# Four changes to the opening of a fused attention and two-layer feed-forward kernel

## The chip, the core and the metric

The kernel runs on one core of a Trainium2 chip. Its engines are TensorE (PE in the profile; PEld is its weight load), VectorE (DVE), ScalarE (ACT), GpSimd (POOL) and SyncE (SP), which here only issues DMAs. The metric is the device time of one execution in microseconds (us). Fewer are better.

## What is computed

Four batches of eight heads of attention with a learned decay, 576 positions of 64, then two feed-forward blocks over the 2304 tokens.

```python
def attention(q, k, v, f):                       # (4, 8, 576, 64), f: (4, 8, 576)
    scores = (1 / sqrt(64)) * (q @ k.T)
    cum = cumsum(log(clip(f, 1e-4, 1)))          # running sums along the sequence
    scores = where(causal, -1e9, scores + cum[:, None] - cum[None, :])
    attn = exp(scores - max(scores))
    return (attn / (sum(attn) + 1e-9)) @ v

x = attention(q, k, v, f)                        # as 2304 tokens x 512
h = ((x @ w1) * (x @ w2)) @ w3                   # 512 -> 1024 -> 1024
x = h @ w_out                                    # 1024 -> 512
h = x @ w_in                                     # 512 -> 2048
out = (h - tanh(h)) @ w_out2                     # 2048 -> 512
```

The weights arrive as float64, so each weight unit has to be turned to float32 on the chip, and each large product is made of three matmuls on a high and a low part of both sides.

## The kernel before, in words

Every step is declared to a planner (`Plan`, `declare`) with its engine, an assumed duration, what it reads and writes and a priority `pr`; the planner runs through them once and writes out one fixed order for each engine. The priorities come from the table `C` (line 38) through `PR`: `a0` to `a3` place the 16 attention pairs, `o0`, `o1`, `w0`, `w1`, `v0`, `v1` the weight units of the first layer, `s0`, `s1` those of the second layer that are converted ahead and spilled to DRAM, `b0` the last eight. Instructions of an engine run in that order, and SP's DMAs too: a DMA that has to wait holds those behind it.

*Running sums.* Line 219 on: `f` for 32 heads is loaded on 32 partitions, clipped, passed through the logarithm and summed by a scan into the tile `PT`; line 240 writes the 32 rows to the DRAM tile `cumd`.

*Attention.* A pair is two heads of a batch (`pair`, `scores`). For each pair SP loads q and k (`qk`, line 356, two buffers), V (`VF`, line 465, two buffers) and the running sums of each head, broadcast from `cumd` to 128 partitions (`cumb`, line 358, one buffer for each head). The scores of a head are five row blocks, each up to the diagonal, in four groups of matmuls (`smm`, line 373). DVE adds the sums and takes the minimum of a row (`smin`, line 388), ACT takes the exponential (line 393), PE transposes (line 444), ACT copies the result out of PSUM (line 449), and PE multiplies by V (line 493). The causal mask is made in two ways: for pairs below `nm` = 9 by two or one more matmuls a row block and head, of the tables `eye` and `trh` (18 a pair), and from pair 9 on by GpSimd, which adds the table `tri` to the diagonal blocks of `cumb` (line 378, ten a pair).

*Weight units.* `conv` (from line 290) turns one unit, 128x512, from float64 to float32: SP loads 512 KB into a raw buffer (`w64`, line 299), ACT takes the absolute of one half (line 309), DVE makes four steps on it (lines 314 to 320), ACT rounds the high part (line 337), and the low part is a subtraction (line 340) on the engine that `lo_eng` names. The first 40 units are those of the first layer: 8 of `wo`, 16 of `w3`, 16 of `w1` and `w2`. With `lod` = 1, the first has its low part on DVE, the others on GpSimd. The raw buffers are a ring of `NW` = 2; with `xu` = 0 the four more that lie in tiles idle at first (`f`, and the second halves of `xy`) are not used. The second and third unit wait for the write of `cumd` (`h0` = 1).

*Matrix work.* `mphase` multiplies `w3` and `wo` into one matrix (192 matmuls of 512 columns), `block1` makes the first layer in six blocks of 384 tokens, between the attention of batches 1, 2 and 3, and the rest is the second layer in five blocks. In the first layer's time the attention of later pairs is woven between.

Of the kernel before, what the change touches and what calls it, by code (L numbers as in the profile page):

```python
# [37 lines left out]
C = {"nb": 4, "nm": 9, "gs": 0.4, "xs": 4, "xu": 0, "wl": 8.0, "h0": 1, "ys": 0.15, "a0": 4.51, "a1": 30.92, "a2": 85.05, "a3": 48.14, "o0": 1.62, "o1": 3.44, "w0": 22.93, "w1": 6.0, "m0": 138.47, "v0": 144.48, "v1": 5.72, "s0": 1059.48, "s1": 9.02, "lod": 1, "evd": 11, "b0": 1268.43, "k0": 1009.76}  # L38
# [32 lines left out]
class Plan:  # L71
# [8 lines left out]
    def op(self, eng, dur, fn, r=(), w=(), pr=0.0, grp=None, after=(), pn=128, use=1.0, lk=False, mode="f", lat=0.0):  # L80


        if eng == "S":
            i = self._op("S", 0.52 if pn == 128 else 0.69, fn, r, w, pr, grp, after)
            return self._op("Q", dur / 360e3 * (128 / max(pn, 64) if pn > 8 else 1), None, r, w, pr, grp, (i,))
        return self._op(eng, dur, fn, r, w, pr, grp, after, use, lk or eng == "P", mode, lat)
# [21 lines left out]
    def schedule(self):  # L108
# [19 lines left out]
        while done < n:  # L128
# [21 lines left out]
            if e == "E":  # L150
                if o["mode"] != mode:
                    t, mode = t + 0.1, o["mode"]
# [48 lines left out]
def declare(P, nc, T, a):  # L201

    op = P.op
# [42 lines left out]
    def consts(z):  # L246
        t = T["J"][:, 128 * z:128 * z + 128] if z < 2 else T["J"][:, 256:512]
        if z == 0:
            G.memset(t, 1.0)
            G.affine_select(t, t, pattern=[[1, 128]], compare_op=ALU.is_equal, fill=0.0, base=0, channel_multiplier=-1)  # L250
        elif z == 1:
            G.memset(t, 0.0)
            G.affine_select(t, t, pattern=[[-1, 128]], compare_op=ALU.is_ge, fill=-1e30, base=0, channel_multiplier=1)
        elif z == 2:
            V.tensor_copy(T["idr"], T["J"][:, 0:128])
        elif z == 3:
            V.tensor_copy(T["tri"], T["J"][:, 128:256])
        elif z == 4:
            V.tensor_copy(T["eye"][0:64, 64:128], T["J"][0:64, 0:64])
            V.tensor_copy(T["eye"][64:128, 64:128], T["J"][64:128, 64:128])  # L260
        elif z == 5:
            V.tensor_copy(T["trh"][0:64], T["J"][0:64, 128:256])
            V.tensor_copy(T["trh"][64:128, 0:64], T["J"][64:128, 192:256])
        elif z == 6:
            V.tensor_copy(T["trh"][64:128, 64:128], T["J"][64:128, 256:320])
        elif z == 7:
            G.memset(t[:, 0:64], -1e30)
            G.memset(t[:, 64:128], 0.0)
        else:
            V.tensor_copy(T["eye"][:, 0:64], T["J"][:, 320:384])  # L270
            V.tensor_copy(T["eye"][:, 128:192], T["J"][:, 320:384])

    for z in range(2):
        op("P", 0.7, lambda z=z: consts(z), w=[f"J.{z}", "J"], pr=-100, grp="att")
        op("D", 0.2, lambda z=z: consts(2 + z), r=[f"J.{z}"], w=["J", ("idr", "tri")[z]], pr=-98, grp="att")
    op("P", 0.4, lambda: consts(7), w=["J.2", "J"], pr=-100, grp="att")
    op("D", 0.3, lambda: consts(4), r=["J.0"], w=["J", "eye"], pr=-98, grp="att")
    op("D", 0.3, lambda: consts(5), r=["J.1"], w=["J", "trh"], pr=-98, grp="att")
    op("D", 0.15, lambda: consts(6), r=["J.2"], w=["J", "trh"], pr=-98, grp="att")
    op("D", 0.3, lambda: consts(8), r=["J.2"], w=["J", "eye"], pr=-98, grp="att")  # L280
# [3 lines left out]
    cnt = [0, 0]  # L284
    borrowed = []
    NW = 2

    def conv(unit, hi, lo, pr, spill=None, reload=None, lo_eng="P", grp=None):
# [63 lines left out]
    def scores(p, t0, o):  # L352
# [3 lines left out]
        o("S", 589824, lambda: Y.dma_start(T[qk], a["qk"][p]), t0 - 20, w=[qk])  # L356
        for y in range(2):
            o("S", 294912, lambda y=y: Y.dma_start(T[f"cumb{y}"], T["cumd"][h + y:h + y + 1].to_broadcast([128, S])), t0 - 8 + 2 * y, r=["cumd"], w=ck[y])
        pem = p < C["nm"]

        def smm(banks, pieces):
            for i, c0, c1, at in pieces:
                d = 128 * i - c0
                n = min(128, S - 128 * i)
                ops = [(lambda k: k[:, :, :].rearrange("p a b -> p (a b)")[:, 128 * i:128 * i + 128], lambda k: k[:, 1, c0:c1], 0, c1 - c0, qk)]
# [4 lines left out]
                for z, (l, r, f, w, src) in enumerate(ops):  # L370
                    for y in range(2):
                        sl = slice(64 * y, 64 * y + 64)
                        E.matmul(T[banks[y]][:, at + f:at + f + w], l(T[src])[sl], r(T[src])[sl], start=z == 0, stop=z == len(ops) - 1)  # L373
# [459 lines left out]
```

## Time and profile before

| | us |
|---|---|
| median of 3 runs | 966.0 (965.81 to 968.46) |
| the profiled execution | 968.27 |
| its span, first to last instruction | 966.6 |
| PE busy in it | 940.6 |
| DVE busy | 630.3 |
| ACT busy | 532.3 |
| POOL busy | 264.1 |

The profile is of one execution. Busy time counts a wait of a matmul inside the array as well, so PE's share is an upper bound of what it does. A row of the timeline gives start and duration of an instruction, or of several alike that are merged; a row of the chain gives start, duration and what was on the path that ended last. The span is 1.7 us shorter than the time of the execution that it is from.

### The profile page before, as it was taken

The numbers are of one execution on the slowest core, as the hardware profiler recorded it, in microseconds if no ns is written. First come the engines' busy times: TensorE is split into PE (matmuls) and PEld (weight loads), VectorE is DVE, ScalarE is ACT, GpSimd is POOL, SyncE is SP. The second block draws the span as 40 slices with busy tenths as digits, with TensorE's granted clock in tenths as the row PEclk, the third lists the DMA queues.
The fourth block names the chain that finished last, engine by engine and source line by source line (L and its number), as shares of the span: only waits on it lengthen the run. The fifth ranks groups of instructions, "written<-read, shape, count | busy, mean of one in ns | idle before, by whom it ended". The sixth has DMA issues, their size and how long they took to land.

```text
span 966.6 us, 14863 instructions
## 1 busy us (share of the span) xinstructions
PE 940.6 (97%) x5314; PEld 797.6 (83%) x5314; DVE 630.3 (65%) x1332; ACT 532.3 (55%) x1170; POOL 264.1 (27%) x251
## 2 busy tenths in 40 slices
PE   5799999999999999999999999999999999999998
PEld 3466777988888988899999988888888888888898
DVE  6698888886777664326422369677568666756675
ACT  4676676665564554433324465655556555655564
POOL 0322332321211111102124457242225223222221
PEclk9999999999999999999999999999999999999999
DMA  5656554546557652003113331011001000100010
GB/s 181 226 182 212 183 188 162 190 152 226 194 195 258 214 184 68 30 13 95 58 58 96 99 120 55 1 44 43 1 1 35 32 1 0 44 1 1 1 44 23
DMA packets 38666, 94.50 MB, mean 98 GB/s; under 512 B 4608, under 2 KB 8832, under 8 KB 38592
## 3 DMA queue, kind: packets, MB, share of 16 engines
q1 hardware_dynamic: 38592, 93.56, 29.0%
q8 instruction: 41, 0.67, 0.3%
q14 instruction: 33, 0.27, 0.1%
HBM read 77.67 MB, written 15.88 MB: 97 GB/s over the span
## 4 chain that ended last, share of the span: by engine, by line
PE 89%; DMA 6%; DVE 2%; ACT 1%; issue 1%; SPq 0%; ACTq 0%; DVEq 0%
PE b L207 26%; PE b L208 25%; PE b L209 25%; PE b L373 5%; PE b L444 4%; PE b L493 3%; DMA w<-in_w_dram 2%; DMA w<-in_wo_dram 1%; DMA rb<-dr 1%; DMA w<-in_win_dram 1%; DMA cumb<-cumd 1%; DMA cumd<-PT 1%; ACT w L309 0%; DVE P L388 0%; DVE w L318 0%
## 5 line engine op out<-in xcount | busy, mean ns | idle before, releaser
L683 POOL TENSOR_TENSOR s<-xy,s 128x512 fp32r<-128x512 f32 (+1 forms) x80 | 99.4, 1243 | 256.3 <-ACT s L682 242.5
L674 DVE SCALAR_TENSOR_TENSOR xy<-b,xy 128x512 f32<-128x512 f32 (+1 forms) x80 | 50.8, 635 | 114.4 <-ACT xy L673 113.2
L679 ACT ACTIVATE xy<-xy,small 128x512 f32<-128x512 f32 (+1 forms) x80 | 54.6, 682 | 79.8 <-DVE xy L678 79.6
L373 PE MATMUL b<-qk 64*128 64x512 f32 (+4 forms) x384 | 80.9, 498 | 11.4 <-DVE small L388 5.7
L449 ACT COPY PT<-b 128x512 f32<-128x512 f32 (+3 forms) x144 | 60.3, 444 | 50.0 <-PE b L444 49.6
L393 ACT ACTIVATE P<-P,small 128x512 f32<-128x512 f32 (+3 forms) x128 | 71.1, 557 | 29.2 <-DVE small L388 28.8
L378 POOL TENSOR_TENSOR cumb<-cumb,tri 128x128 f32<-128x128 f32 (+1 forms) x70 | 35.6, 513 | 162.3 <-DVE small L388 122.0
L682 ACT CAST s<-xy 128x512 fp32r<-128x512 f32 (+1 forms) x80 | 46.1, 577 | 60.3 <-DVE xy L681 60.3
L388 DVE CUSTOM_DVE_ANT_0 P<-b,cumb 128x512 f32<-128x512 f32 (+3 forms) x128 | 60.0, 483 | 24.0 <-PE b L373 22.4
L559 DVE TENSOR_TENSOR f<-b,f 128x384 f32<-128x384 f32 x48 | 26.5, 553 | 71.0 <-PE b L209 65.5
L309 ACT ACTIVATE w<-w 128x512 f32<-128x512 f32 x72 | 48.5, 673 | 36.9 <-DMA w<-in_wo_dram 16.6
L681 DVE COPY_PREDICATED xy<-xy 128x512 f32<-128x512 uint32 (+1 forms) x80 | 61.5, 769 | 9.3 <-ACT xy L679 2.4
L678 DVE SCALAR_TENSOR_TENSOR xy<-xy 128x512 f32<-128x512 f32 (+1 forms) x80 | 65.5, 818 | 0.0
L680 DVE SCALAR_TENSOR_TENSOR xy<-xy 128x512 f32<-128x512 f32 (+1 forms) x80 | 60.3, 754 | 6.8
L314 DVE TENSOR_SCALAR w<-w 128x512 f32<-128x512 f32 x72 | 33.6, 466 | 45.9 <-ACT w L309 45.3
L444 PE MATMUL b<-idr,P 128*128 128x128 f32 x320 | 53.2, 285 | 8.2 <-ACT PT L449 4.6
L373 PEld LDWEIGHTS b<-qk 64*128 64x128 f32 x384 | 35.3, 198 | 30.0 <-issue 8.9
L444 PEld LDWEIGHTS b<-idr,P 128*128 128x128 f32 x320 | 39.3, 144 | 24.6 <-ACT PT L449 11.5
L672 ACT ACTIVATE xy<-b 128x512 f32<-128x512 f32 (+1 forms) x80 | 44.5, 556 | 26.7 <-PE b L209 25.8
L318 DVE SCALAR_TENSOR_TENSOR w<-w,w 128x512 uint32<-128x512 uint32 x72 | 56.0, 779 | 1.0
L676 ACT ACTIVATE xy<-xy,small 128x512 f32<-128x512 f32 (+1 forms) x80 | 54.7, 683 | 0.0
L320 DVE SCALAR_TENSOR_TENSOR w<-w,w 128x512 uint32<-128x512 uint32 x72 | 53.5, 746 | 0.7
(630 smaller groups left out, 2839.8 us busy)
## 6 DMA issues: line engine op xcount, KB each, us to landing
w<-in_wo_dram SPq DMA_DIRECT2D x24, 512.0 KB
qk<-in_qk_dram SPq DMA_DIRECT2D x16, 576.0 KB
cumb<-cumd SPq DMA_DIRECT2D x32, 288.0 KB
w<-in_w3t_dram SPq DMA_DIRECT2D x16, 512.0 KB
w<-in_w_dram SPq DMA_DIRECT2D x16, 512.0 KB
w<-in_win_dram SPq DMA_DIRECT2D x16, 512.0 KB
VF<-in_v_dram SPq DMA_DIRECT2D x16, 320.0 KB
rb<-dr SPq DMA_DIRECT2D x32, 144.0 KB
```

The costliest lines, as they stand in the source:

```text
L207: E.matmul(o, lh, rh, start=start, stop=False)
L208: E.matmul(o, lh, rl, start=False, stop=False)
L209: E.matmul(o, ll, rh, start=False, stop=stop)
L373: E.matmul(T[banks[y]][:, at + f:at + f + w], l(T[src])[sl], r(T[src])[sl], start=z == 0, stop=z == len(ops) - 1)
L388: V.tensor_tensor_reduce(out=out, in0=T[b][0:qn, at:at + c1 - c0], in1=T[cum][0:qn, c0:c1], scale=-0.125, scalar=3e38, op0=ALU.add, op1=AL ...
L393: A.activation(t, t, AF.Exp, bias=T["MX"][:, z:z + 1], scale=-1.0, accum_out=T["SM"][:, z:z + 1])
L444: E.transpose(T[tb][0:n, 128 * z:128 * z + 128], T[src][:, c:c + n], T["idr"].bitcast(F32))
L449: (A.copy if ev == "A" else V.tensor_copy)(out(), src)
L678: op("D", d_dve(nb), lambda w=w, u=u, v=v, nb=nb: V.scalar_tensor_tensor(v(w), v(u), -P_ROOT, v(w), ALU.add, ALU.mult), r=[u], w=[w], lk=T ...
L680: op("D", d_dve(nb), lambda w=w, vv=vv, v=v, nb=nb: V.scalar_tensor_tensor(v(w), v(vv), P_D, v(w), ALU.add, ALU.mult), r=[vv], w=[w], lk=T ...
L681: op("D", d_dve(nb), lambda w=w, u=u, th=th, v=v, nb=nb: V.copy_predicated(v(w), v(u).bitcast(U32), v(th)), r=[u, th], w=[w], lk=True, **pa)
L683: op("P", d_pool(nb), lambda w=w, gh=gh, gl=gl, v=v, nb=nb: G.tensor_sub(v(gl), v(w), v(gh)), r=[w, gh], w=[gl], pr=pa["pr"], after=[*pa[" ...
```

## The change

It replaces the planner's constants and makes four changes to the program.

The two broadcasts of pair 0 read the running sums from `PT` in SBUF, one partition each, instead of from `cumd`; the loads of q and k for pair 1 and of V for pairs 0 and 1 are put behind them in SP's order (`held`). The first 20 weight units use a ring of six raw buffers (`xu` = 20, `xs` = 4), and no unit waits for the sums any more. The masks of all pairs are made by GpSimd with a select on the diagonal blocks of `cumb`; the mask matmuls, and the tables `tri`, `eye` and `trh`, are gone. The low parts of the first 40 units are all on DVE (`lod` = 40). The planner's own assumptions change too: a broadcast counts 2.7 times its bytes, the queue has 400 instead of 360 GB/s, a change of matmul type costs 0.17 instead of 0.1 us.

```diff
-C = {"nb": 4, "nm": 9, "gs": 0.4, "xs": 4, "xu": 0, "wl": 8.0, "h0": 1, "ys": 0.15, "a0": 4.51, "a1": 30.92, "a2": 85.05, "a3": 48.14, "o0": 1.62, "o1": 3.44, "w0": 22.93, "w1": 6.0, "m0": 138.47, "v0": 144.48, "v1": 5.72, "s0": 1059.48, "s1": 9.02, "lod": 1, "evd": 11, "b0": 1268.43, "k0": 1009.76}
+C = {"nb": 4, "gs": 0.928, "xs": 4, "xu": 20, "wl": 8.0, "h0": 3, "ys": 0.2, "a0": 3.061, "a1": 18.261, "a2": 74.699, "a3": 41.761, "o0": 1.714, "o1": 3.421, "w0": 22.93, "w1": 8.714, "m0": 145.732, "v0": 91.41, "v1": 4.532, "s0": 1167.053, "s1": 10.311, "lod": 40, "evd": 11, "b0": 1479.445, "k0": 1009.76}
...
-            return self._op("Q", dur / 360e3 * (128 / max(pn, 64) if pn > 8 else 1), None, r, w, pr, grp, (i,))
+            return self._op("Q", qx * dur / 400e3 * (128 / max(pn, 64) if pn > 8 else 1), None, r, w, pr, grp, (i,))
...
+    held = []
...
-            op("S", 524288, load, w=[k64], pr=pr - C["wl"], grp="w64", after=(cumw,) if C["h0"] < cnt[0] < 4 else ())
+            op("S", 524288, load, w=[k64], pr=pr - C["wl"], grp="w64", after=held if C["h0"] < cnt[0] < 4 else ())
...
-        o("S", 589824, lambda: Y.dma_start(T[qk], a["qk"][p]), t0 - 20, w=[qk])
+        o("S", 589824, lambda: Y.dma_start(T[qk], a["qk"][p]), t0 - 20, w=[qk], after=held if p == 1 else ())
         for y in range(2):
-            o("S", 294912, lambda y=y: Y.dma_start(T[f"cumb{y}"], T["cumd"][h + y:h + y + 1].to_broadcast([128, S])), t0 - 8 + 2 * y, r=["cumd"], w=ck[y])
-        pem = p < C["nm"]
+            if p:
+                o("S", 294912, lambda y=y: Y.dma_start(T[f"cumb{y}"], T["cumd"][h + y:h + y + 1].to_broadcast([128, S])), t0 - 8 + 2 * y, r=["cumd"], w=ck[y], qx=2.7)
+            else:
+                held.append(len(P.ops))
+                o("S", 294912, lambda y=y: Y.dma_start(T[f"cumb{y}"], T["PT"][y:y + 1, 0:1, 0:S].to_broadcast([1, 128, S])), -300 + y, r=ok, w=ck[y], qx=2.7)
...
-                if pem and c1 > 128 * i:
-                    ops.append((lambda k: k[:, 64:192], lambda k: T["trh"][:, 0:n], d, n, "eye"))
-                    if n > 64:
-                        ops.append((lambda k: k[:, 0:128], lambda k: T["trh"][:, 0:64], d + 64, 64, "eye"))
...
-            G.tensor_tensor(t, t, T["tri"].bitcast(F32)[0:qn, 0:qn], op=ALU.add)
+            G.affine_select(t, t, pattern=[[-1, qn]], compare_op=ALU.is_ge, fill=-1e30, base=0, channel_multiplier=1)
...
-                    if (i, c0) != (4, 0) and not pem:
-                        o("P", 0.55, lambda y=y, i=i: mask(y, i), ty, r=["tri"], w=[ck[y][i]])
+                    if (i, c0) != (4, 0):
+                        o("P", 0.32, lambda y=y, i=i: mask(y, i), ty, w=[ck[y][i]])
...
-        o("S", 327680, lambda: Y.dma_start(T[VF], a["v"][p]), -12, w=[VF])
-
         scores(p, -2.0, o)
+        o("S", 327680, lambda: Y.dma_start(T[VF], a["v"][p]), -12, w=[VF], after=held if p < 2 else ())
```

## Rows read from the trace of the kernel before

**Rows 1.** The page's part 1: busy us (share of the span) xinstructions.
```profile
PE 940.6 (97%) x5314; PEld 797.6 (83%) x5314; DVE 630.3 (65%) x1332; ACT 532.3 (55%) x1170; POOL 264.1 (27%) x251
```

**Rows 2.** Stages: stretch, its length, busy us of each engine, clock, DMA, GB/s.
```profile
core 0: us, PE busy (x) PEld busy (x) DVE busy (x) ACT busy (x) POOL busy (x), PEclk, DMA share, GB/s
0.00:75.00 75.00, 55.89 (x369) 38.42 (x370) 56.50 (x172) 48.25 (x123) 16.81 (x21) 0.98 0.58 196
75.00:200.00 125.00, 122.31 (x801) 95.86 (x801) 109.09 (x269) 86.05 (x218) 36.48 (x26) 1.00 0.55 183
200.00:450.00 250.00, 249.47 (x1610) 219.40 (x1607) 151.98 (x426) 124.24 (x326) 42.32 (x76) 1.00 0.44 148
```

**Rows 3.** PE's waits in the whole span: us in total, times, longest.
```profile
PE b L373 <- DVE small L388: 5.7, 2, 5.5
PE b L373 <- DMA qk<-in_qk_dram: 5.6, 1, 5.6
```

**Rows 4.** The timeline's first 26 us: start, duration, engine, line, operation.
```profile
1.08 0.29 POOL L250 TENSOR_SCALAR_AFFINE_SELECT J<-J 128x128 f32<-128x128 f32 x1
...
6.08 0.33 SPq L240 DMA_DIRECT2D cumd<-PT  x1
...
9.69 0.43 DVE L316 TENSOR_SCALAR w<-w 128x512 uint32<-128x512 uint32 x1
10.15 0.69 DVE L318 SCALAR_TENSOR_TENSOR w<-w,w 128x512 uint32<-128x512 uint32 x1
...
10.97 0.81 SPq L358 DMA_DIRECT2D cumb<-cumd  x2
...
12.25 0.69 DVE L340 TENSOR_TENSOR A0l<-w,A0h 128x512 fp32r<-128x512 f32 x1 [0.68 <-ACT A0h L337]
14.44 0.68 DVE L388 CUSTOM_DVE_ANT_0 J<-b,cumb 64x512 f32<-64x512 f32 x1 [1.49 <-DMA cumb<-cumd]
...
16.32 0.68 DVE L388 CUSTOM_DVE_ANT_0 J<-b,cumb 64x512 f32<-64x512 f32 x1 [0.58 <-DMA cumb<-cumd]
...
25.19 1.23 PE L373 MATMUL b<-qk 64*128 64x512 f32 x2
```

**Rows 5.** The stages' view of 5 to 10 us, columns as in rows 2.
```profile
5.00:10.00 5.00, 4.05 (x12) 1.87 (x12) 1.77 (x6) 1.01 (x3) 0.00 (x0) 1.00 0.90 326
```

**Rows 6.** The page's part 3: the DMA queue's packets, MB and share.
```profile
q1 hardware_dynamic: 38592, 93.56, 29.0%
```

**Rows 7.** Waits of DVE and of ACT from 0 to 200 us.
```profile
DVE w L314 <- ACT w L309: 13.7, 15, 3.2
...
ACT w L309 <- DMA w<-in_wo_dram: 7.8, 5, 3.2
```

**Rows 8.** The stages' view of line 340 alone: DVE busy, POOL busy.
```profile
0.00:75.00 75.00, 0.69 (x1) 15.48 (x11) 0.98 0.58 196
75.00:200.00 125.00, 0.00 (x0) 36.48 (x26) 1.00 0.55 183
```

**Rows 9.** DVE's groups by line, 75 to 200 us: count, busy us, mean ns.
```profile
L318 DVE SCALAR_TENSOR_TENSOR w<-w,w 128x512 uint32<-128x512 uint32 x27 | 23.5, 872 | 0.3
L320 DVE SCALAR_TENSOR_TENSOR w<-w,w 128x512 uint32<-128x512 uint32 x26 | 19.4, 745 | 0.1
L316 DVE TENSOR_SCALAR w<-w 128x512 uint32<-128x512 uint32 x27 | 15.0, 555 | 0.2
```

**Rows 10.** The chain that ended last, in order of time: start, us, what.
```profile
112.56 1.20 PE b L373 x8
...
117.58 1.32 PE b L373 x14
...
122.99 1.22 PE b L373 x16
...
222.73 1.06 PE b L373 x4
...
226.50 1.01 PE b L373 x8
...
232.74 0.85 PE b L373 x8
```

More of the change, by code (lines that the diff above doesn't have):

```diff
@@ L78, in __init__, with op @@
         self.readers = {}
-    def op(self, eng, dur, fn, r=(), w=(), pr=0.0, grp=None, after=(), pn=128, use=1.0, lk=False, mode="f", lat=0.0):
+    def op(self, eng, dur, fn, r=(), w=(), pr=0.0, grp=None, after=(), pn=128, use=1.0, lk=False, mode="f", lat=0.0, qx=1.0):
         if eng == "S":
             i = self._op("S", 0.52 if pn == 128 else 0.69, fn, r, w, pr, grp, after)
-            return self._op("Q", dur / 360e3 * (128 / max(pn, 64) if pn > 8 else 1), None, r, w, pr, grp, (i,))
+            return self._op("Q", qx * dur / 400e3 * (128 / max(pn, 64) if pn > 8 else 1), None, r, w, pr, grp, (i,))
         return self._op(eng, dur, fn, r, w, pr, grp, after, use, lk or eng == "P", mode, lat)
@@ L151, in schedule @@
                 if o["mode"] != mode:
-                    t, mode = t + 0.1, o["mode"]
+                    t, mode = t + 0.17, o["mode"]
                 while t >= (win + 1) * HAM:
@@ L246, in consts @@
     def consts(z):
-        t = T["J"][:, 128 * z:128 * z + 128] if z < 2 else T["J"][:, 256:512]
+        t = T["J"][:, 0:128]
         if z == 0:
@@ L250, in consts @@
             G.affine_select(t, t, pattern=[[1, 128]], compare_op=ALU.is_equal, fill=0.0, base=0, channel_multiplier=-1)
[L251 to L268, printed above, removed]
-        else:
[L270 to L280, printed above, removed]
+        else:
+            V.tensor_copy(T["idr"], t)
+    op("P", 0.5, lambda: consts(0), w=["J"], pr=-100, grp="att")
+    op("D", 0.2, lambda: consts(1), w=["J", "idr"], pr=-98, grp="att")
     op("D", 0.15, lambda: V.memset(T["J"][:, S:640], 0.0), w=["J"], pr=-98, grp="att")
     cnt = [0, 0]
+    held = []
     borrowed = []
@@ L355, in scores @@
         ck = [[f"cumb{y}.{z}" for z in range(5)] for y in range(2)]
-        o("S", 589824, lambda: Y.dma_start(T[qk], a["qk"][p]), t0 - 20, w=[qk])
+        o("S", 589824, lambda: Y.dma_start(T[qk], a["qk"][p]), t0 - 20, w=[qk], after=held if p == 1 else ())
         for y in range(2):
-            o("S", 294912, lambda y=y: Y.dma_start(T[f"cumb{y}"], T["cumd"][h + y:h + y + 1].to_broadcast([128, S])), t0 - 8 + 2 * y, r=["cumd"], w=ck[y])
-        pem = p < C["nm"]
+            if p:
[3 more added lines that the diff above has]
+                o("S", 294912, lambda y=y: Y.dma_start(T[f"cumb{y}"], T["PT"][y:y + 1, 0:1, 0:S].to_broadcast([1, 128, S])), -300 + y, r=ok, w=ck[y], qx=2.7)
         def smm(banks, pieces):
             for i, c0, c1, at in pieces:
-                d = 128 * i - c0
-                n = min(128, S - 128 * i)
-                ops = [(lambda k: k[:, :, :].rearrange("p a b -> p (a b)")[:, 128 * i:128 * i + 128], lambda k: k[:, 1, c0:c1], 0, c1 - c0, qk)]
-                if pem and c1 > 128 * i:
-                    ops.append((lambda k: k[:, 64:192], lambda k: T["trh"][:, 0:n], d, n, "eye"))
-                    if n > 64:
-                        ops.append((lambda k: k[:, 0:128], lambda k: T["trh"][:, 0:64], d + 64, 64, "eye"))
[L370 to L373, printed above, removed]
+                for y in range(2):
+                    sl = slice(64 * y, 64 * y + 64)
+                    E.matmul(T[banks[y]][:, at:at + c1 - c0], T[qk].rearrange("p a b -> p (a b)")[sl, 128 * i:128 * i + 128], T[qk][sl, 1, c0:c1],
+                             start=True, stop=True)
         def mask(y, i):
@@ L398, in scores @@
             banks = [ring("s%d" % len(names), names) for _ in range(2)]
-            du = sum(1.04 * d_f32(c1 - c0) + (0.2 if pem and c1 > 128 * i else 0) for i, c0, c1, at in pieces)
-            o("E", du, lambda banks=banks, pieces=pieces: smm(banks, pieces), t, r=[qk] + (["trh", "eye"] if pem else []), w=banks, mode="r")
+            du = sum(1.04 * d_f32(c1 - c0) for i, c0, c1, at in pieces)
+            o("E", du, lambda banks=banks, pieces=pieces: smm(banks, pieces), t, r=[qk], w=banks, mode="r")
             for y in range(2):
@@ L765, in tile_kernel @@
     add(ap, "J", [128, 640], F32)
-    add(ap, "eye", [128, 192], F32R)
-    add(ap, "trh", [128, 128], F32R)
     for i in range(2):
@@ L772, in tile_kernel @@
     add(ap, "rb", [128, S], F32)
-    add(ap, "tri", [128, 128], F32R)
     add(ap, "idr", [128, 128], F32R)
```

## The prediction

> **What bounds the kernel now.** I read the page's first part, then the busy time by stage, then the waits of the engine that bounds. TensorE (PE) is busy for 940.6 of 966.6 us [rows 1], so the time can fall only where PE idles, where PE does work that can be dropped, or where it is "busy" with little in hand. By stages [rows 2] the three differ. From 0 to 75 us PE is busy for 55.9 of 75; VectorE (DVE) is busy for 56.5, and ScalarE for 48.3, so here PE waits for what the other engines prepare. From 75 to 200 us PE is at 122.3 of 125 and DVE at 109.1 of 125: both are nearly full. From 200 to 450 us PE is at 249.5 of 250 while DVE has 98 us to spare. After that PE has no wait in the list that matters, and nothing in this change takes work from it. PE's longest waits are two, both at the start: 5.6 us for the first q/k load, and 5.7 us in two waits for DVE's score pass [rows 3]. The time has to be won before 200 us, and DVE is the engine to watch there.
>
> The sum is made against the profiled execution: span 966.6 us, its own time 968.27, which lies inside the three runs and 2.3 above their median of 966.0. I take the difference in us from the profile and apply it to the median.
>
> **First broadcast.** Before, the running sums go out to DRAM at 6.08, and the two broadcasts are issued at 10.97, when that write has landed; DVE's first score pass starts at 14.44 (head 0) and its first of head 1 at 16.32 [rows 4]. After, the broadcast needs only the sums in SBUF, so SP can issue it at about 6.1: 4.9 us sooner. But SP has one queue, and the change also puts more ahead of it. Six raw-weight buffers are free at time zero and no unit is held any more (h0 = 3 leaves no unit that satisfies 3 < n < 4), so SP issues q/k of pair 0 (576 KB) and six units of 512 KB while it waits for the sums. That is 0.59 + 6 x 0.524 = 3.74 MB. Early in the kernel the queue moves 326 GB/s [rows 5], so it drains in 11.5 us, at about 13.5 us. The broadcast follows; if it costs what the one from DRAM costs (10.97 to 14.44, and 1.9 more for the second), less the latency that now overlaps, it lands at about 15 and 16.5. So I cost this step at nothing: it is swallowed by the loads in front of it. q/k of pair 1 and V of pairs 0 and 1 move behind it, 1.25 MB or 3.8 us at that rate, and land near 20; pair 1's scores start at 25.19 [rows 4], which hides them, with 5 us of cover. What the trace does not show is a broadcast whose source is one SBUF partition. Its bounds come from the queue's row [rows 6]: 29.0% of 16 engines' span over 38592 packets is 0.116 us a packet of 2.4 KB, so 128 rows take 0.93 us if all 16 engines work side by side and 14.9 us if the one partition serves one packet at a time. I take the low end, because the DRAM broadcast also reads one row 128 times and is near it. The high end is rival A.
>
> [...]
>
> **Raw-weight buffers.** In the first 200 us DVE waits 13.7 us for ScalarE's first step on a unit, and ScalarE in turn for the unit's load [rows 7]. With two buffers a load cannot start until the unit before last is done. Six buffers for the first 20 of 40 units, which cover about the first 100 us, can remove some 9 us of that. Also, DVE is mostly idle early, 1.77 us busy of the 5 from 5 to 10 us [rows 5]; by 13.5 us it can have two or three units done where before it had one.
>
> **Low parts on DVE.** 11 low parts in the first stage and 26 in the second leave GpSimd, where they took 15.5 and 36.5 us [rows 8], for DVE, which did the one it had in 0.69 us [rows 4]: +7.6 and +17.9 us of DVE. Against that, the unit's other DVE steps are slower while GpSimd runs. In 75 to 200 us they take 872, 745 and 555 ns [rows 9]; alone, at 9.7 to 10.9 us, they took 0.69, 0.69 (that of L318 stands for both) and 0.43 [rows 4]. That is 0.18 + 0.06 + 0.12 = 0.36 us a unit, 9.5 us over 26 units, if all of it comes back, and nothing if it does not; I take most of it, as GpSimd will have only short work left. In the first stage the same difference is small, about 2 us.
>
> **Masks.** PE loses the mask matmuls of pairs 0 to 8. In the chain, three score groups of a masked pair take 1.20 + 1.32 + 1.22 = 3.74 us and the same three of an unmasked one 1.06 + 1.01 + 0.85 = 2.92 [rows 10]: 0.82 us a pair, and the fourth group has no mask. For pairs 4 to 8, which lie where PE is full, that is 4.1 us off the end; for pairs 0 to 3 it is 3.3 us inside a stage where PE waits anyway, so it counts there or not at all. GpSimd gets ten selects a pair instead, at 0.29 us each [rows 4]. In the second stage that is 5 x 10 x 0.29 = 14.5 us where it now has 36.5 of low parts, so it has room. A score pass now waits for its select after the broadcast lands; the first group of row block 4 needs none and takes 0.68 us on DVE, which hides two selects. If it does not, a pair loses under 1 us of DVE order, which other DVE work fills. The constant tables that vanish are 8 copies of about 0.2 us at 3 to 4 us, while DVE waits for the logarithm: nothing.
>
> **The rest of the order.** The planner's constants move whole groups: pairs 0 to 3 closer together, the second layer's spill conversions later. The spills go to a stage where DVE has room (98 us before 450) and PE is never short. I cost this at zero, within 3 us.
>
> **Sum.** First stage: DVE's 56.5 + 7.6 - 2 - 1 = 61 us of work, with an idle share that falls from 18.5 to about 9, ends near 70 instead of 75: -5 us (bounds -12, and +1 if the idle share stays where it is). Masks of pairs 4 to 8: -4. Second stage: DVE's demand is 109.1 + 17.9 - 9.5 = 117.5 us in a stage that should shrink to 121; at 97% it cannot keep all of PE's gain, +2 (bounds 0 and +9). Broadcast: 0 (bounds -1 and +14). In all -7, so 966.0 - 7 = 959. The forecast's own range is 948 to 963.
>
> [...] At the high bound the broadcasts land at 13.5 + 14.9 = 28 and at 43 us, 27 us later for head 1 than before, and everything in the queue behind waits too. DVE uses the first part of that wait for its six units (0.43 + 0.43 + 0.69 + 0.69 and the low part's 0.69 make 2.9 us, six are 17 [rows 4]), so about half of the delay is lost: +14 on the forecast, 973, slower than before. By that slope of one half it turns from gain to loss when head 1's sums land 14 us later than I expect, near 30 us, or from 8 us a broadcast. For it: no row shows such a source. Against it: the DRAM broadcast of one row runs near the parallel bound. Chance 0.28; it gives 961 to 976.
>
> **Rival B: DVE becomes the bound and the gain stays in the first stage.** If the slowed steps don't get back what GpSimd took, DVE needs 127 us between 75 and 200, where PE could be through in 121. Then the second stage ends some 7 us later than forecast, and what the buffers won is given back: 966, no change. For it: DVE is already at 87% there, and only half of the units have deep buffers. Against it: GpSimd's long operations do go. Chance 0.22; it gives 961 to 970.
>
> **How the numbers follow.** Forecast 0.50. Faster or slower means by over 0.3%, 2.9 us, about what a measurement of this kernel can tell from no change: below 963.1 or above 968.9. The forecast is almost all faster (0.49), A one part in six faster, one in five no change, the rest slower (0.04, 0.06, 0.18), B a third faster and over half no change (0.08, 0.12, 0.02). That makes 0.61 faster, 0.19 no change, 0.20 slower. The range 948 to 972 leaves out A's upper end and the forecast's lowest part.
>
> **What would show it.** Of the changed kernel: DVE's first pass on the scores near 15 us (A: 25 or later, with PE idle before it); no mask matmuls, and score groups of 1.06, 1.01 and 0.85 us from pair 0 on; DVE over 90% busy from 20 to 200 us with the unit's two-input steps near 0.69 us (B: still 0.75 to 0.87); PE full from about 70 us. The forecast is wrong if the first sums land after 30 us, if DVE's steps on a unit don't get faster, or if PE shows a new wait after 450 us, where I allow none.

## The result: 974 us, 6 to 7 us slower

| median, us | before | after |
|---|---|---|
| both kernels side by side, 4 runs each | 967.08 (965.81 to 968.46) | 974.20 (973.14 to 974.71) |
| span of the profiled execution | 966.6 | 973.0 |

The ratio is 1.006, interval 1.0037 to 1.0083. The forecast was 959, and 974.2 lies above its range; it is rival A's time (973) within 1.2 us.

The profile of after, page parts 1 and 3 and the row of the clock (columns as in [rows 1] and [rows 6]):

```profile
PE 932.6 (96%) x5152; PEld 785.5 (81%) x5152; DVE 630.8 (65%) x1363; ACT 531.7 (55%) x1170; POOL 241.3 (25%) x298
...
PEclk7699999999999999999999999999999999999999
...
q1 hardware_dynamic: 39360, 93.56, 30.6%
```

PE has 162 matmuls fewer (9 pairs x 18) and 8.0 us less to do than in [rows 1], and still the span is 6.4 us longer. The stages' view of after says where (columns as in [rows 2]):

```profile
0.00:75.00 75.00, 42.39 (x220) 25.76 (x221) 48.57 (x144) 40.13 (x99) 15.15 (x36) 0.80 0.79 203
75.00:200.00 125.00, 121.87 (x744) 91.07 (x743) 113.23 (x311) 88.44 (x231) 25.88 (x55) 1.00 0.53 170
200.00:450.00 250.00, 248.97 (x1615) 218.32 (x1614) 158.00 (x438) 128.86 (x337) 33.00 (x80) 1.00 0.46 154
```

Against [rows 2], PE's busy time falls by 13.5 us in the first stage, by 0.4 in the second and by 0.5 in the third. So PE has been busy for 14.4 us less by 450 us. 8.0 of that is work that is gone; the other 6.4 are the whole growth of the span. Nearly all of it is lost in the first stage. The waits of PE in the whole span, and of DVE from 0 to 200 us (us in total, times, longest):

```profile
PE b L343 <- DVE small L359: 23.2, 5, 13.9
PE b L343 <- DMA qk<-in_qk_dram: 5.5, 1, 5.5
...
DVE J L359 <- DMA cumb<-PT: 15.7, 2, 8.1
DVE w L290 <- ACT w L285: 9.3, 9, 1.8
```

PE's wait for DVE's score pass grew from 5.7 us [rows 3] to 23.2. DVE's own wait behind it is new: 15.7 us, for the two broadcasts out of `PT`. The timeline of after (SP's and DVE's rows; x2 merges two instructions):

```profile
5.85 1.17 SPq L338 DMA_DIRECT2D cumb<-PT  x2
...
17.79 13.22 SPq L275 DMA_DIRECT2D w<-in_wo_dram  x2
...
22.24 0.68 DVE L359 CUSTOM_DVE_ANT_0 J<-b,cumb 64x512 f32<-64x512 f32 x1 [7.61 <-DMA cumb<-PT]
...
32.08 0.68 DVE L359 CUSTOM_DVE_ANT_0 J<-b,cumb 64x512 f32<-64x512 f32 x1 [8.11 <-DMA cumb<-PT]
```

SP issued the broadcasts at 5.85, 5.1 us sooner than in [rows 4], as the change says. The first passes came at 22.24 and 32.08, where before had 14.44 and 16.32 [rows 4]. They lie 9.84 us apart, so one broadcast of 0.295 MB moves at 30 GB/s. The stages' view of that stretch:

```profile
0.00:14.00 14.00, 3.60 (x8) 1.18 (x8) 8.49 (x20) 6.94 (x10) 0.70 (x6) 0.94 0.89 283
14.00:32.00 18.00, 1.64 (x2) 0.49 (x2) 2.33 (x6) 0.32 (x1) 0.93 (x2) 0.50 0.89 57
```

From 14 to 32 us the DMA engines are as busy as before it (0.89) and move a fifth as much, 57 GB/s. SP's next two weight loads take from 17.79 to 31.01; issuing the first of them alone lasts 12.57 us. And all engines stand: PE is busy for 1.64 of 18 us, DVE for 2.33.

### The profile page after: what moved, and what is told of

Read it like the earlier page. It is cut to its first block, busy times and chain, and to the rows that moved or that the text cites. A ratio compares the mean times of both kernels' runs of the same rounds, so it can differ in the third digit from the quotient of the medians.

```text
span 973.0 us, 14824 instructions
## 1 busy us (share of the span) xinstructions
PE 932.6 (96%) x5152; PEld 785.5 (81%) x5152; DVE 630.8 (65%) x1363; ACT 531.7 (55%) x1170; POOL 241.3 (25%) x298
## 3 DMA queue, kind: packets, MB, share of 16 engines
q1 hardware_dynamic: 39360, 93.56, 30.6%
## 4 chain that ended last, share of the span: by engine, by line
PE 82%; DMA 9%; ACT 4%; DVE 3%; issue 1%; SPq 1%; DVEq 0%; ACTq 0%
PE b L207 24%; PE b L208 24%; PE b L209 24%; PE b L343 4%; PE b L415 3%; PE b L463 3%; DMA cumb<-PT 3%; DMA rb<-dr 2%; ACT P L364 1%; DMA w<-in_w_dram 1%; ACT PT L420 1%; DMA dr<-VF 1%; ACT w L285 1%; DMA w<-in_win_dram 1%; DMA w<-in_wo_dram 1%
## 5 line engine op out<-in xcount | busy, mean ns | idle before, releaser
L349 POOL TENSOR_SCALAR_AFFINE_SELECT cumb<-cumb 128x128 f32<-128x128 f32 (+1 forms) x160 | 68.0, 426 | 337.3 <-DVE small L359 220.8
L343 PE MATMUL b<-qk 64*128 64x512 f32 (+4 forms) x384 | 77.3, 486 | 28.8 <-DVE small L359 23.2
L364 ACT ACTIVATE P<-P,small 128x256 f32<-128x256 f32 (+3 forms) x128 | 71.1, 557 | 36.4 <-DVE small L359 35.7
L420 ACT COPY PT<-b 128x512 f32<-128x512 f32 (+2 forms) x144 | 59.8, 445 | 46.2 <-PE b L415 45.7
L285 ACT ACTIVATE w<-w 128x512 f32<-128x512 f32 x60 | 40.3, 674 | 35.2 <-DMA w<-in_w_dram 11.7
L290 DVE TENSOR_SCALAR w<-w 128x512 f32<-128x512 f32 x72 | 31.0, 434 | 35.6 <-ACT w L285 35.1
L647 DVE TENSOR_TENSOR xy<-b,xy 128x512 f32<-128x512 f32 (+1 forms) x80 | 50.2, 627 | 2.5 <-ACT xy L643 2.5
L463 PE MATMUL b<-PT,VF 128*64 128x288 f32 (+3 forms) x448 | 46.5, 357 | 0.0
```

Source lines behind the costliest of these rows:

```text
L343: E.matmul(T[banks[y]][:, at:at + c1 - c0], T[qk].rearrange("p a b -> p (a b)")[sl, 128 * i:128 * i + 128], T[qk][sl, 1, c0:c1], start=Tru ...
L349: G.affine_select(t, t, pattern=[[-1, qn]], compare_op=ALU.is_ge, fill=-1e30, base=0, channel_multiplier=1)
L364: A.activation(t, t, AF.Exp, bias=T["MX"][:, z:z + 1], scale=-1.0, accum_out=T["SM"][:, z:z + 1])
L420: (A.copy if ev == "A" else V.tensor_copy)(out(), src)
L463: E.matmul(T[bank][64 * y:64 * y + 64, c0 - q0:288], T[VF][:, j, y], r, start=j == 0, stop=j == js[-1])
```

## The experiments

Three theories stood after the result. Theory 1: the broadcast from one partition is slow and its delay is the loss, while the rest of the sum holds. Theory 2: the broadcast only shows where the loss is, and the new order, or DVE's added work, is its cause. Theory 3: six loads ahead of it in the queue are to blame. The kernels either keep an order (that of before or after, with the instructions named moved) or are planned anew, which the text says each time.

### The broadcast

**after_dram** keeps the order of after; pair 0 reads `cumd` again, and the write of `cumd` goes ahead of it.

```diff
-T["PT"][y:y + 1, 0:1, 0:S].to_broadcast([1, 128, S])
+T["cumd"][h + y:h + y + 1].to_broadcast([128, S])
...
+        order.remove(P.cumd)
+        order.insert(order.index(P.first[0]), P.cumd)
```

> The changed kernel with its order kept on every engine, except that SP writes the sums to DRAM first and pair 0's two broadcasts then come from there, as before the change. Theory 1 (the one-partition source is the loss): DVE's first score passes of the two heads start near 16 and 18 us instead of 22.2 and about 31.5, PE stays at the high clock from 25 us on, and the time falls by most of the 14 us that head 1 comes sooner, to 957 to 963. Theory 2 (the six units that DVE converts meanwhile cover the late sums, and the rest of the change is what costs): the first passes come just as early, but the time stays at 968 or above.

Measured: 961.68 where before has 968.86, ratio 0.9918 (0.9901 to 0.9936). Its timeline:

```profile
5.85 0.45 SPq L241 DMA_DIRECT2D cumd<-PT  x1
...
13.87 0.81 SPq L340 DMA_DIRECT2D cumb<-cumd  x2
...
18.26 0.68 DVE L361 CUSTOM_DVE_ANT_0 J<-b,cumb 64x512 f32<-64x512 f32 x1 [3.20 <-DMA cumb<-cumd]
20.02 0.68 DVE L361 CUSTOM_DVE_ANT_0 J<-b,cumb 64x512 f32<-64x512 f32 x1
```

Two transfers, the write and the read back, beat one from SBUF by 4.0 us for head 0 and 12.1 us for head 1, and the kernel is 12.5 us faster than after by the medians, 13.7 by the two ratios to before. So the broadcast's source turns the change from a gain to a loss.

**after_spread** keeps SBUF as the source and the order of after, but lays the sums of each head on 32 partitions; each broadcast is four copies from 32 partitions to 32.

```diff
+[Y.dma_start(T["rb"][32 + 32 * y:64 + 32 * y], a["f"][y:y + 1].to_broadcast([32, S])) for y in range(2)]
...
-T["PT"][y:y + 1, 0:1, 0:S].to_broadcast([1, 128, S])
+[Y.dma_start(T[f"cumb{y}"][32 * z:32 * z + 32], T["PT"][32 + 32 * y:64 + 32 * y, 0, 0:S]) for z in range(4)]
```

> The changed kernel in its own order, still from SBUF and without DRAM, but the sums of heads 0 and 1 are made on 32 partitions each (two more small loads of f), and each broadcast is four copies of 32 partitions to 32. Theory 1: it is the single partition that is slow, not SBUF as a source; a broadcast takes 1 to 2.5 us instead of 9.2, the first passes start near 16 and 18 us, the time is 957 to 963, like the one with the DRAM source. Theory 2: SBUF to SBUF is slow as such: the passes start after 20 us and the time stays at 970 or above.

Measured: 960.37 (before 968.86), ratio 0.9923 (0.9898 to 0.9947). Its timeline:

```profile
17.19 0.68 DVE L359 CUSTOM_DVE_ANT_0 J<-b,cumb 64x512 f32<-64x512 f32 x1 [1.03 <-DMA cumb<-PT]
18.95 0.68 DVE L359 CUSTOM_DVE_ANT_0 J<-b,cumb 64x512 f32<-64x512 f32 x1
```

The second head follows 1.76 us after the first instead of 9.84. Neither here nor in after_dram does DVE wait for the second head, so 1.76 is an upper bound for the transfer. So it is not SBUF as a source that is slow, but 128 reads of one partition. The order and DVE's added work are those of after: theory 2 falls.

**before_sbuf** has the order of before and takes from the change the broadcast alone.

```diff
-T["cumd"][h + y:h + y + 1].to_broadcast([128, S])
+T["cumd"][h + y:h + y + 1].to_broadcast([128, S]) if p else T["PT"][y:y + 1, 0:1, 0:S].to_broadcast([1, 128, S])
...
+        for i in P.first:
+            order.remove(i)
+            order.insert(order.index(P.cumd), i)
```

> The kernel before in its own order, with this one part of the change: pair 0's broadcasts come from one partition of SBUF each, ahead of the write of the sums to DRAM. Theory 1: behind 2.36 MB of loads they land near 20 and 29 us, 13 us later than before for head 1, and the weight loads behind them are as late; the time rises by 8 to 13 us, to 975 to 980. Theory 2: other work covers it: 966 to 970.

Measured: 983.91 (before 968.86), ratio 1.015 (1.0125 to 1.0175). Its timeline:

```profile
19.98 0.68 DVE L393 CUSTOM_DVE_ANT_0 J<-b,cumb 64x512 f32<-64x512 f32 x1 [8.07 <-DMA cumb<-PT]
...
29.90 0.68 DVE L393 CUSTOM_DVE_ANT_0 J<-b,cumb 64x512 f32<-64x512 f32 x1 [8.62 <-DMA cumb<-PT]
```

Here one weight unit, not six, stands ahead of it in SP's queue (2.36 MB of loads in all instead of 3.74), and the two passes are again 9.9 us apart: theory 3 falls. Head 1's pass is 13.6 us later than in [rows 4], and the kernel 15 us slower, more than theory 1 expected. PE's granted clock stays high here while the broadcasts run (the stages' view):

```profile
0.00:25.00 25.00, 5.69 (x14) 2.36 (x14) 8.43 (x26) 5.55 (x8) 1.32 (x10) 1.00 0.87 117
25.00:50.00 25.00, 17.86 (x112) 12.84 (x112) 15.11 (x46) 13.27 (x36) 4.37 (x3) 1.00 0.56 154
```

So the loss does not need the low clock that after has from 14 us on (0.50).

**after_known_cost** asks whether the delay can be lived with: after, with the planner told what the broadcast costs, and planned anew.

```diff
-..., r=ok, w=ck[y], qx=2.7)
+..., r=ok, w=ck[y], qx=12.6)
```

> The changed kernel with its one-partition broadcasts, where the planner is told what they take (9.3 us each, a factor of 12.6 on the bytes instead of 2.7) and plans anew; nothing else differs. Theory 1 (a good part of the loss is DVE's fixed order: in the changed kernel it idles 15.7 us for the sums with half-done units right behind): DVE finishes all six units before head 1's pass, idles under 8 us for the sums, and the time is 965 to 969. Theory 2 (the loss is attention that starts late, whatever DVE does meanwhile): still 972 to 975.

Measured: 975.07 (before 969.03), ratio 1.0062 (1.0044 to 1.0079). Its first stage, DVE's wait, and PE's two largest waits behind the passes:

```profile
0.00:75.00 75.00, 45.95 (x230) 27.96 (x230) 54.87 (x154) 44.22 (x104) 13.02 (x36) 0.95 0.82 216
...
DVE J L359 <- DMA cumb<-PT: 5.1, 2, 4.0
...
PE b L415 <- ACT P L364: 17.2, 2, 16.9
...
PE b L343 <- DVE small L359: 6.0, 6, 3.8
```

DVE now works through the wait: 54.87 us busy instead of 48.57, waiting 5.1 us instead of 15.7. PE's granted clock stays at 0.95 where it was 0.80. The time doesn't move. Head 1's first pass starts at 32.10, as late as in after (32.08), and PE's waits for score passes and for the exponentials behind them come to 23.2 us, as much as after's wait for DVE. So filling DVE's wait did not bring the attention forward. The late start of the attention is the reading that fits; as this order is a new one, and an order has a price of its own (below), the run alone does not show it.

**after_own_sums** goes the other way: `f` itself is loaded to 128 partitions for both heads, and the sums are made there, with no broadcast (planned anew).

```diff
+        op("S", 294912, lambda y=y: Y.dma_start(T[f"cumb{y}"], a["f"][y:y + 1].to_broadcast([128, S])), w=c0, pr=-215 + y, grp="att")
+        (clip, Ln, scan and a factor of -8 on cumb, on 128 partitions)
```

> The changed kernel, planned anew, with no broadcast of sums for pair 0 at all: f of heads 0 and 1 is loaded to all 128 partitions and clipped, passed through the logarithm and summed there (about 2.9 us of DVE and ScalarE for each head, at a time when both idle). Theory 1: the first passes start at 8 to 11 us, some 12 and 20 us sooner than in the changed kernel, and the time is 950 to 958, below both kernels. Theory 2: 965 or above, since the early start finds no unit of weights ready and DVE is the bound anyway.

Its time, 961.84, lies between the two theories.

**after_dram_three_loads** and **after_spread_three_loads** take the kernels above and put three of the six first loads behind the broadcasts.

```diff
+        for i in P.loads[3:6][::-1]:
+            order.remove(i)
+            order.insert(order.index(P.first[1]) + 1, i)
```

> The kernel of the run with the DRAM source, with only three of the six raw-weight loads ahead of the sums in SP's order and the other three right behind the broadcasts. Theory 1 (the sums of that run, at 18.3 us, are late because the write and the broadcast stand behind 3.7 MB): the write lands near 9 us, the first score passes start near 12.5 and 14 us, and since attention is what PE lives on in the first stage, the time falls by 2 to 4 us, to 957 to 960. Theory 2 (DVE is the bound of that stage, and only its order changes): within 1.5 us of 961.7.

> The run with the spread SBUF source, with three of the six raw-weight loads behind the broadcasts. Theory 1 (what is ahead of the sums in the queue decides when they land, and an earlier start is worth something): first passes at 12 to 14 us instead of 17.2, time 956 to 960. Theory 2 (once the sums land before about 20 us, the first stage is bound by DVE's and ScalarE's work): 959.5 to 962, like the runs with the DRAM and the spread source.

| | first passes at, us | median | before | ratio |
|---|---|---|---|---|
| after_own_sums | 11.01, 12.07 | 961.84 | 968.86 | 0.9925 (0.9908 to 0.9943) |
| after_dram_three_loads | 14.65, 17.38 | 961.19 | 969.18 | 0.9929 (0.9905 to 0.9954) |
| after_spread_three_loads | 15.73, 17.85 | 961.71 | 969.03 | 0.993 (0.9899 to 0.996) |
| after_spread | 17.19, 18.95 | 960.37 | 968.86 | 0.9923 (0.9898 to 0.9947) |
| after_dram | 18.26, 20.02 | 961.68 | 968.86 | 0.9918 (0.9901 to 0.9936) |
| after | 22.24, 32.08 | 974.20 | 967.08 | 1.006 (1.0037 to 1.0083) |

Nothing clear of the intervals is won here by sums that come before about 20 us for head 1, and from there to after's 32 each microsecond costs about one (12.5 to 13.7 us for 12.1). In the order of before, the mean price from 16.32 on is about the same (15 for 13.6); where it begins there was not tried. Own sums was planned anew, so its row also holds what a new order is worth (below).

### The masks and the low parts

**before_lo_dve** (order of before; first 40 low parts on DVE):

```diff
-(G if lo_eng == "P" else V).tensor_sub(...)
+(G if lo_eng == "P" and n_lo > 40 else V).tensor_sub(...)
```

> The kernel before in its own order, with this one part of the change: the low parts of the first 40 units on DVE instead of GpSimd, at their places in the order. Theory 1 (the prediction's term: DVE takes 26 us more and gets back about 12 from its own steps, which no longer run beside GpSimd): the unit's two-input steps fall to about 0.69 us between 75 and 200 us, DVE goes from 87% to over 92% busy there, and the time is 0 to 4 us longer, 967 to 972. Theory 2 (the low part on GpSimd is on the path of the next product, 1.3 to 1.8 us against 0.69): it is shorter, 960 to 966.

Measured: 968.12 (before 969.18), ratio 0.9997 (0.9977 to 1.0017). DVE's groups, 75 to 200 us (count, busy us, mean ns):

```profile
L318 DVE SCALAR_TENSOR_TENSOR w<-w,w 128x512 uint32<-128x512 uint32 x27 | 18.6, 687 | 0.2
L320 DVE SCALAR_TENSOR_TENSOR w<-w,w 128x512 uint32<-128x512 uint32 x27 | 18.5, 686 | 0.1
...
L316 DVE TENSOR_SCALAR w<-w 128x512 uint32<-128x512 uint32 x27 | 11.4, 421 | 0.2
```

All of the forecast relief came: 872, 745 and 555 ns [rows 9] are now 687, 686 and 421, 0.38 us a unit. DVE's busy time in the stage rose by 2.8 us only, and the time did not move.

**before_selects** (order of before; each select issued just ahead of its score pass, no mask matmuls):

```diff
-                if pem and c1 > 128 * i:
+                if False:
...
-            G.tensor_tensor(t, t, T["tri"].bitcast(F32)[0:qn, 0:qn], op=ALU.add)
+            G.affine_select(t, t, pattern=[[-1, qn]], compare_op=ALU.is_ge, fill=-1e30, base=0, channel_multiplier=1)
...
+            if pem and (i, c0) != (4, 0):
+                mask(y, i)
```

> The kernel before in its own order, with this one part of the change: the masks of all pairs by GpSimd selects, each just ahead of its score pass, and no mask matmuls (162 fewer). Theory 1: PE's 4.1 us of pairs 4 to 8 come off and half of the 3.3 us of the first four, 961 to 964. Theory 2: GpSimd's low parts, 1.3 to 1.8 us each, stand ahead of selects in its order, DVE's score passes wait for them, and the gain is lost: 966 to 970.

Measured: 975.80 (before 969.18), ratio 1.0077 (1.0052 to 1.0101). The masks alone make the kernel slower, and by more than either theory had. DVE's waits from 0 to 200 us:

```profile
DVE P L390 <- POOL cumb L378: 20.3, 27, 1.8
...
DVE J L390 <- POOL cumb L378: 3.5, 3, 1.6
```

A select stands behind a low part on GpSimd, up to 1.8 us, and the score pass behind the select: 23.8 us of waits.

**before_selects_lo_dve** joins the two edits above, in the order of before. 

> The kernel before in its own order, with two parts of the change: the selects, each just ahead of its score pass, and the low parts of the first 40 units on DVE. Theory 1 (selects cost only behind low parts on the same engine): DVE waits under 6 us for GpSimd instead of 23.8, and the time is 958 to 966, so the two parts gain only together. Theory 2 (a select is in the chain from sums to score pass, whoever is ahead of it): 971 to 977, as with the selects alone.

Measured: 967.0 (before 969.38), ratio 0.9978 (0.9955 to 1.0001). Its DVE waits:

```profile
DVE P L392 <- POOL cumb L380: 5.4, 13, 2.2
```

The waits fall from 23.8 to 5.4 us and the time by 8.8, to 1 us above theory 1. In this order the selects need the low parts off GpSimd, and the two together gain about 2 us, with an interval that reaches no change.

**after_dram_pe_masks** (order of after_dram; pairs 0 to 8 masked by PE again, with the tables):

```diff
+                if p < 9 and c1 > 128 * i:
+                    (the mask matmuls of before)
...
+            p < 9 or G.affine_select(...)
```

> The run with the DRAM source, in its order, with the masks of pairs 0 to 8 back on PE (162 mask matmuls, the tables made at the start) and no selects for these pairs. Theory 1 (the prediction's term: 0.82 us a pair of PE, 4.1 to 7.4 us in all): 965 to 969. Theory 2 (the first 200 us are bound by DVE and by waits, PE has room for the mask matmuls): 960 to 963.

Measured: 969.08 (before 969.38), ratio 0.9994 (0.9968 to 1.002). Against after_dram's 961.68 that is 7.4 us, by the ratios as well, and nine pairs at 0.82 make 7.4. The intervals leave it open by some 3 us either way, and PE's busy time in the two profiles differs by 5.2 us (938.7 and 933.5), so the match to the tenth is chance; five pairs alone, 4.1, lie just outside.

**after_dram_lo_gpsimd** (order of after_dram; low parts of units 2 to 40 on GpSimd):

```diff
-(G if lo_eng == "P" else V).tensor_sub(...)
+(G if lo_eng == "P" or 1 < n_lo <= 40 else V).tensor_sub(...)
```

> The kernel of the run with the DRAM source (the changed kernel in its own order, pair 0's sums broadcast from DRAM), with the low parts of units 2 to 40 back on GpSimd at their places in the order. Theory 1 (the low parts on DVE cost little or nothing and free the selects' engine): the time is 962 to 967, no better than the 961.7 of that run, as selects now queue behind low parts. Theory 2 (DVE is the bound from 20 to 200 us, so each 0.69 us on it counts): 950 to 958.

Measured: 964.03 (before 969.18), ratio 0.9955 (0.994 to 0.997): 2.4 us above after_dram by the medians, 3.6 by the ratios. DVE's groups from 75 to 200 us are slow again; the last row is its wait for selects from 0 to 200 us, 0.2 us in after_dram:

```profile
L296 DVE SCALAR_TENSOR_TENSOR w<-w,w 128x512 uint32<-128x512 uint32 x22 | 20.0, 911 | 0.1
L294 DVE TENSOR_SCALAR w<-w 128x512 uint32<-128x512 uint32 x26 | 17.3, 673 | 0.2
L298 DVE SCALAR_TENSOR_TENSOR w<-w,w 128x512 uint32<-128x512 uint32 x22 | 16.5, 751 | 0.1
...
DVE P L363 <- POOL cumb L353: 2.4, 4, 1.4
```

In this order, where the planner has placed the selects, selects and low parts share GpSimd at a price of 2.4 us of waits, not 23.8, and the kernel is still faster than before.

### The order, and the buffers

These kernels are planned anew. **before_selects_planned** is before with all masks as selects (`nm` 9 to 0); **before_six_buffers** has `xu` 0 to 20; **before_slow_sums** has the planner's new assumptions alone (2.7 for broadcasts, 400 GB/s, 0.17); **before_six_buffers_slow_sums** has both of the last two. **after_dram_planned** is the program of after_dram in the order that the planner gives it, and **after_dram_two_buffers** is that with two raw buffers:

```diff
-"nm": 9, ... o("P", 0.55, lambda y=y, i=i: mask(y, i), ty, r=["tri"], w=[ck[y][i]])
+"nm": 0, ... o("P", 0.32, lambda y=y, i=i: mask(y, i), ty, w=[ck[y][i]])
...
-"xu": 0        (before_six_buffers)
+"xu": 20
...
-dur / 360e3 ... t + 0.1        (before_slow_sums)
+qx * dur / 400e3 ... t + 0.17
...
+..., r=["cumd"], w=ck[y], qx=2.7)        (after_dram_planned, source cumd)
...
-"xu": 20        (after_dram_two_buffers)
+"xu": 0
```

> The kernel before, planned anew with its old constants, with all masks by GpSimd selects and the mask matmuls gone; the planner places the selects as early as the sums allow. Theory 1 (the selects cost only where they stand behind low parts, which took 23.8 us of DVE's time in the run with each select just ahead of its pass): DVE waits under 5 us for GpSimd, and the 162 dropped matmuls show: 960 to 965. Theory 2 (selects on GpSimd beside low parts cost what the matmuls save): 967 to 972.

> The kernel before, planned anew with its old constants, with six raw-weight buffers for the first 20 units instead of two. Theory 1: DVE's waits for a unit's first step, 13.7 us from 0 to 200, fall below 7, and the time falls by 3 to 6 us, to 961 to 965. Theory 2 (PE and the attention chain set the first stage): 966 to 969.

> The kernel before, unchanged but for the planner's three new assumptions, planned anew. Theory 1 (they matter only with deep buffers): within 3 us of the kernel before, 966 to 972. Theory 2 (they are worth something by themselves, as DVE waits less for sums): 958 to 964.

> The kernel before with six raw-weight buffers, planned anew with the old constants and the new planner's assumptions (a broadcast counts 2.7 times its bytes, 400 GB/s, 0.17 us for a change of matmul type). Theory 1 (six buffers alone cost because loads stand ahead of later pairs' sums, for which DVE waited 11.7 us in that run; told of dearer broadcasts, the planner issues them sooner): DVE's waits for sums fall below 5 us and the time is 962 to 969. Theory 2 (the old constants don't suit six buffers): still above 974.

> The changed kernel with pair 0's sums broadcast from DRAM, planned anew for it (the earlier run with the DRAM source kept the old order). Both theories: 959 to 965, near the 961.7 of that run; it is the base for the next.

> The same with two raw-weight buffers for all units, as in the kernel before (xu = 0), planned anew. Theory 1 (the prediction's term of about 5 us): 965 to 970, with DVE's waits for a unit's first step back at 13 us or more in the first 200. Theory 2 (deep buffers put loads ahead of sums and give PE nothing, as the two runs with them alone showed): 955 to 962.

| | median | before | ratio |
|---|---|---|---|
| before_selects_planned | 975.91 | 969.03 | 1.0073 (1.0045 to 1.0102) |
| before_six_buffers | 979.83 | 969.03 | 1.0121 (1.0091 to 1.015) |
| before_slow_sums | 973.63 | 969.38 | 1.0041 (1.0019 to 1.0063) |
| before_six_buffers_slow_sums | 983.41 | 969.38 | 1.0144 (1.01 to 1.0188) |
| after_dram_planned | 968.23 | 967.46 | 1.0012 (0.9992 to 1.0033) |
| after_dram_two_buffers | 969.15 | 967.46 | 1.0018 (0.9995 to 1.0042) |

Four of the six lie outside both of their theories: before_selects_planned, before_six_buffers, before_slow_sums and after_dram_planned. After_dram_two_buffers lies in theory 1's range, but so does its base by now. The planner's assumptions alone cost about 4 us.

In before_selects_planned, DVE's wait for selects from 0 to 200 us is short, as theory 1 had it:

```profile
DVE P L388 <- POOL cumb L378: 1.7, 1, 1.7
```

The time is still 975.91, that of before_selects with its 23.8 us of waits. So these waits are not shown to be the whole price of the selects in before's order; here the loss may be the new order's.

after_dram_planned and after_dram do the same work, and the new order costs 6.5 us by the medians, 9.1 by the ratios. So a part that is seen only in a new order can't be priced to better than that. In part it is the sums again: the new order puts two more weight loads ahead of the broadcast. The first passes of head 1 in after_dram_planned, with six buffers, and in after_dram_two_buffers:

```profile
22.65 0.68 DVE L359 CUSTOM_DVE_ANT_0 J<-b,cumb 64x512 f32<-64x512 f32 x1
...
15.43 0.68 DVE L359 CUSTOM_DVE_ANT_0 J<-b,cumb 64x512 f32<-64x512 f32 x1
```

After_dram has 20.02. Two buffers or six differ by 0.9 us, inside both intervals, but they differ in these 7 us of the first sums too, so this pair does not price the buffers alone. The six buffers alone cost before 11 us. The DVE waits of before_six_buffers, from 0 to 200 us:

```profile
DVE w L314 <- ACT w L309: 15.2, 12, 4.4
DVE J L388 <- DMA cumb<-cumd: 11.7, 5, 5.9
```

The wait that the buffers were to remove is there still (13.7 us before [rows 7]), and one for running sums has come. That looked like loads that crowd out the sums. But with the sums counted as slow the wait fell to 6.1 us and the time did not come back (983.41). In both orders the longest of these waits, 5.9 and 5.6 us, is that for pair 0, whose head 1 starts at 19.9 us instead of 16.3; at one microsecond for each, that is a quarter to a third of the loss. What makes the six buffers so dear in these two orders stays open.

## Why the prediction was wrong

**The step that failed is the price of the first broadcast.** The text bounded it by 0.93 and 14.9 us and took the low end, "because the DRAM broadcast also reads one row 128 times and is near it". The source in DRAM is no model for a source in one partition: 1.76 us against 9.84 from one head to the next. With this step undone, and nothing else, the forecast's sign and size are back (after_dram 961.7, 7.2 below before; forecast 7 below). The two bounds held the cost but lay far apart, and nothing in the trace of before stood near the low one for this kind of source. The picture behind the high one was not right either: the rows are not read one at a time at 0.116 us but side by side at 1.25 us each (last section). Rival A, the high bound at 0.28, should have been the forecast. The queue in front was well forecast: the first slow row starts at 12.2 us in after's trace, 13.5 in the text. Why one partition is slow no run here shows: between one source partition (9.84 us) and 32 (at most 1.76) nothing was tried.

**What is late next** was also mis-sized. Rival A took a slope of one half, since six units fill DVE's wait. Measured, it is about one (12.5 us for 12.1; before_sbuf 15 for 13.6), and filling DVE's wait gave nothing back in the new order of after_known_cost. That rival A gave 973 all the same came from two errors that meet: 27 us at a slope of one half there, 12.1 us (over after_dram) at one here. That the attention's own chain of passes sets the end of the first stage would explain it; this is argued, not shown.

**The broadcast's early issue** was worth nothing, as forecast: SP's queue drained to it late, and first sums at 14.65 us won no more than at 18.26 (at 11 neither, in a new order).

**Masks**: the matmuls' price was right. The score groups in after's chain, pairs after 96 us, against [rows 10]:

```profile
96.49 1.06 PE b L343 x4
...
100.46 1.01 PE b L343 x8
...
104.32 0.85 PE b L343 x8
```

But the masks are worth some 7.4 us instead of 4.1, which speaks for all nine pairs: the text left it open whether pairs 0 to 3 count. And "a pair loses under 1 us of DVE order" holds in the order of after, with 0.2 us of waits for selects from 0 to 200 us, 2.4 with the low parts back on GpSimd. With each select just ahead of its pass, behind low parts, the gain turns into a loss of 7 us (before_selects).

**Low parts on DVE**: the relief was right (0.38 us a unit, 0.36 forecast), the sign of the term was not. It was put down as +2; it is -2 to -4 in after_dram and nothing in the order of before (before_lo_dve). What pays in after_dram, the faster steps or the selects' shorter waits (2.4 us), was not separated. Rival B, that the steps stay slow, is out: in the groups of after the same steps take 684, 689 and 424 ns.

**First stage and buffers**, forecast at -5, showed little of it. (Its upper bound was a wrong sum: 61 us of work and an idle share still at 18.5 end at 79.5, which is +4.5 and not +1.) The stages of after_dram:

```profile
0.00:75.00 75.00, 54.88 (x301) 33.23 (x302) 60.04 (x177) 49.94 (x127) 18.48 (x44) 0.98 0.69 229
75.00:200.00 125.00, 121.71 (x745) 92.91 (x744) 112.11 (x302) 85.78 (x218) 23.75 (x50) 1.00 0.53 171
```

PE is busy for 54.88 us of the first stage, 55.89 in [rows 2]. The masks of pairs 0 to 3, 3.3 us of that, are gone, so PE is about 2 us further on at 75 us, not 5, and the low parts' gain is in that as well. Two buffers or six came to the same in after_dram_planned, with the first sums at different times; in after_dram's own order that was not tried. So of the -7 without the broadcast, which came as -7.2, the parts are others: taken out one at a time, masks -7.4 and low parts -2 to -4. The two act on each other, so they can't simply be added; if they could, 2 to 4 us would be lost by what is left (start, buffers, order). The total was right by luck.

**The order**, costed at zero within 3 us: a new one moves the time by 6.5 us (after_dram_planned), the later first sums included, twice the bound that the text gave it. That the order of after suits this program was not to be seen in the diff.

## What to carry to other kernels

Before a transfer is moved off DRAM, look at how many partitions its source has: here 128 reads of one partition took 9.84 us, and the loads behind them in the same DMA queue waited too (issuing two of them lasted from 17.79 to 31.01 us). If a row must be spread, try it on 32 partitions first, or through DRAM; both beat the two kernels here (after_spread 960.4, after_dram 961.7, before 968.9). Price an unknown transfer by the row that shares its source, not by one that shares its shape. Test parts that use one engine together and look at the order they are issued in: selects behind subtractions on GpSimd cost 23.8 us of waits in one order and 2.4 in another.

## What the hardware showed that I had not expected

Many reads of one partition hold the DMA engines without moving much. After and after_dram have the same 39360 packets in this queue. Its share is 30.6% of 973.0 us in after and 29.5% of 962.0 in after_dram, so the 16 engines spent 16 x (297.7 - 283.8) = 222 us more. The packets of the kept trace say where: of the 320 rows of 2304 bytes in after's first 36 us (256 are those of the two broadcasts), 194 take 1.20 to 1.30 us each, up to 16 of them at once, where after_spread's rows of that size take 0.13 on average and 0.34 at most, and before's 0.11 and 0.44. Eight such rows on each of 16 engines are 10.0 us, near the 9.84 measured. That fits a DMA share that stays at 0.89 while 57 GB/s move, and weights behind that are held as well (SP's next two loads are issued only by 31.01 us).

From 14 to 32 us, with PE busy for 1.64 of 18 us, its granted clock is 0.50; from 0 to 14 us, with 3.60 of 14, it was 0.94. In after_known_cost the first stage has 0.95 instead of 0.80, and the time is the same, in a new order; in before_sbuf, with its order kept, the clock is 1.00 up to 50 us, and the loss is 15 us.
